# Batch 0's q and k in rows of eight tokens: loads, transposes and ordering copies at the start of a fused attention and feed-forward kernel

## The chip, the cores and the metric

The kernel runs on one core of a Trainium2 chip. A core has five engines with queues of their own: TensorE (PE in the profile; its weight loads have a row of their own, PEld), VectorE (DVE), ScalarE (ACT), GpSimd (POOL) and SyncE (SP), and 16 DMA engines that serve transfers issued from POOL, SP and ACT. The metric is the device time of one execution in microseconds (us). The kernel before takes 291.97 us, the median of three runs (291.71 to 292.54).

## The reference

For each of 8 batches and 8 heads there are 576 tokens of 64 values. Scores are masked to a causal window: heads 0 to 3 see the last 32 tokens, heads 4 to 7 ("dilated") every fourth token of the last 128. Softmax, product with v, and then a feed-forward layer over all 4608 tokens:

```
rel = pos[:, None] - pos[None, :]
mask_plain = (rel >= 0) & (rel < 32)
mask_dil = (rel >= 0) & (rel < 128) & (rel % 4 == 0)
attn = softmax(where(mask, q @ k.T / 8, -1e9))      # per batch and head
x = (attn @ v) moved to [4608 tokens, 512]
out = relu(x @ w_in) ** 2 @ w_out                    # 512 -> 2048 -> 512
```

Inputs and output are float32; the kernel computes in bfloat16, and its loads through POOL's queue convert on the way.

## The kernel before, in words

Attention of one batch and the feed-forward products of earlier tokens are interleaved. TensorE is the engine that is kept busy: nearly all of its time goes into the feed-forward products (`mm1`, line 912, with w_in; lines 960 and 997 with w_out), which start as soon as the first 256 tokens of attention output stand in the tile `xT`.

The order of all work is written by hand. The string `PROGRAM` (line 22 on) is read code by code by `run` (line 1147); what stands before its first `|` is issued before any feed-forward group, and each `|` is one feed-forward group further. Every engine runs its instructions in the order in which they were issued and waits on semaphores; a wait holds up all that is queued behind it on that engine.

Batch 0 has its own path, `first_step` (line 678). Its heads come in four pairs e = 0 to 3 (pairs 2 and 3 are dilated) and its tokens in two parts: part 0 is tokens 0 to 255, part 1 tokens 256 to 575. The codes used here:

- `L0:q001` loads part 0 of q and then of k for pairs 0 and 1, through `load_qk` (line 190), on POOL's queue. One row of the staging tile (`rb[0]`, tiles `qb` and `kb` in the profile) holds four consecutive tokens per head: partition p has tokens 4p to 4p+3, 64 partitions for part 0 and 80 for part 1. The order of loads is q001, q023, q123, v0d (two loads of v), i0 (the first quarter of w_in), q101, more of v, i1, more of v, i2, i3 and the four quarters of w_out. From the ninth load on, each waits until the load eight places ahead of it has landed.
- `T e part` (line 706) turns the rows into columns on TensorE: for q and for k, for each of the four tokens r of a row and both heads of the pair, one weight load of 64 or 80 rows by 64 values and one matmul with the identity, 16 transposes in all, into a PSUM tile [128, q or k, r, token/4]. `T20q` and `T20k` are its halves.
- `C e part` (lines 713 to 721) copies that PSUM tile to `xx[0]`: q in the order [r][m] (token 4m + r), k in the same order for the dilated pairs, and for the plain pairs in token order. The letter a or v after the code names ScalarE or VectorE. Because r is the outer index in PSUM too, the copies of line 713 and of line 720 read and write runs of neighbouring elements; that of line 721 does not read so. Line 715 copies the last 64 keys into `k8`.
- `B`, `S`, `E` are the mask added in PSUM (line 736), the scores (line 758) and the exponential (line 766, and the mask on VectorE, line 769); `P`, `D` the product with v and the sums (lines 796, 812); `L`, `X`, `M` the reciprocal of the sums by logarithm and exponential (lines 819, 822 on ScalarE) and the product with it into `xT` (line 829 on VectorE). `G` spreads v (line 255).
- `w` and `W` are products of zeros of 512 or 256 columns (`turn`, line 676) that change no result; they stand at fixed places in TensorE's order.
- `R` (line 925) empties the first two PSUM accumulators of `mm1`, which were held back.
- `y` clears rows 64 to 79 of the staging tiles of batch 1 (`rb[1]`) and of batches 0 and 2 (`rb[0]`), two memsets on POOL each, lines 1150 and 1151.

The plain and dilated pairs of part 0 go first (T00, T10, T20, T30), then part 1 of the dilated pairs (T21, T31), the first two feed-forward groups, then T01 and T11.

Of the kernel before, what the change touches and what calls it, by code (L numbers as in the profile page):

```python
# [12 lines left out]
RES = 4  # L13
# [68 lines left out]
def kernel(  # L82
# [9 lines left out]
    nc = tc.nc  # L92
    P = nc.NUM_PARTITIONS
# [58 lines left out]
    s2 = const.tile([P, HF, HT], bf16, name="s2T")  # L152
    osb = const.tile([P, NT // P, DM], f32, name="osb")
    slots = [0]
    rb = [{nm: const.tile([80, 2 * H * RES * D], bf16, name=f"{nm}b{i}") for nm in "qk"} for i in range(3)]
    qT = const.tile([P, NE, RES, M], bf16, name="qT")

    xx = [const.tile([P, 2, H * 2 * M], bf16, name=f"xx{i}") for i in range(2)]
# [27 lines left out]
    def staged(b: int, nm: str):  # L186


        t = rb[STAGE[b]][nm]
        return t[:, :].rearrange("p (a h x) -> p a h x", h=H, a=2)  # L190

    def load_qk(b: int, part, es):
        hs = slice(2 * es[0], 2 * es[-1] + 2)
# [486 lines left out]
    def first_step(code: str):  # L680
# [16 lines left out]
        if what == "T":  # L697
            if code[3:] != "k":
                ps = ps_a.tile([P, 1024], bf16, name="pa")
                first["T", e, part] = ps[:, 0 : 2 * w].rearrange("p (x r m) -> p x r m", x=2, r=RES)  # L700
            x = first["T", e, part]
            for z, nm in [(z, nm) for z, nm in enumerate("qk") if code[3:] in ("", nm)]:
                t = staged(0, nm)
                for r in range(RES):
                    for hl, rows in enumerate(sides):
                        nc.tensor.transpose(
                            x[rows, z, r, :], t[0:n, part, 2 * e + hl, D * r : D * r + D], ident[0:n, 0:n]
                        )
        elif what == "C":
            copy = nc.scalar.copy if code[3] == "a" else nc.vector.tensor_copy  # L710
            x = first.pop(("T", e, part))
            if dil:
                copy(qk0[:, :, e, :, m0 : m0 + n], x)
                if part:
                    nc.vector.tensor_copy(
                        k8[:, e - NE // 2, :].rearrange("p (m r) -> p m r", r=RES),
                        x[:, 1, :, n - 16 : n].rearrange("p r m -> p m r"),
                    )
            else:
                copy(qk0[:, 0, e, :, m0 : m0 + n], x[:, 0, :, :])  # L720
                nc.vector.tensor_copy(
                    xx[0][:, 1, S * e + RES * m0 : S * e + w + RES * m0].rearrange("p (m r) -> p m r", r=RES),
                    x[:, 1, :, :].rearrange("p r m -> p m r"),
                )
        elif what == "B":
# [421 lines left out]
    def run(code):  # L1147
        if code == "y":
            for nm in "qk":
                nc.gpsimd.memset(staged(1, nm)[64:80, 0, :, :], 0.0)  # L1150
                nc.gpsimd.memset(staged(2, nm)[64:80, 0, 0 : H // 2, :], 0.0)
        elif code == "z":
            nc.gpsimd.memset(vbd[1][0:64, :, :, 64:128], 0.0)
            nc.gpsimd.memset(vbd[1][64:128, :, :, 0:64], 0.0)
        elif code in "mu":
            masks(int(code == "u"))
        elif code == "R":
            while held:
                held.pop(0)()
        elif code == "N":  # L1160
            zero_halves(vbd[0][:, NE // 2 :, 0:8, :])
        elif code[0] == "G":
            spread_v(0, int(code[1]), [int(code[2])], nc.scalar.copy if code[3:] else nc.vector.tensor_copy)
        elif code == "h":
            for rows in sides:
                nc.vector.tensor_copy(vbd[0][rows, 0:2, 0:4, rows], plain[rows, :, :, :])
        elif code == "n":
            zero_halves(kbd)
            nc.sync.dma_start(mask_n[:, :], near_dram.ap())
        elif code[0] in "wW":  # L1170
            n, _, at = code[1:].partition("+")
            turn(int(n), 512 if code[0] == "w" else 256, [int(x) for x in at])
        elif code[0] in "TCBSEPDXM" or code[0] == "L" and code[2:3] != ":":
            first_step(code)
        elif code[0] != "L":
            step(int(code[0]), code[1:])
        else:
            b, what, part, which = int(code[1]), code[3], code[4:5], code[5:]
            if what == "V":
                load_v_rows(b, code[4:] or "d01")  # L1180
                return
            if what == "q":
                load_qk(b, None if part == "w" else int(part), [int(e) for e in which])
            elif what == "x":
                cross_all(b)
            elif what == "v":
                load_v(b, [0, 1] if part == "w" else [int(part)], which)
            else:
                (load_w_in if what == "i" else load_w_out)(int(part))
# [100 lines left out]
```

## Time and profile before

| what | value |
|---|---|
| median of three runs | 291.97 us |
| the profiled execution's own time | 292.3 us |
| its span, first to last instruction | 290.5 us |
| TensorE clock granted | 1.0 throughout |
| TensorE busy, 0 to 4.6 us / 4.6 to 8 / 8 to 12 | 3.53 / 3.08 / 3.50 us |
| 12 to 16 / 16 to 20 / 20 to 24 / 24 to 28 us | 3.02 / 3.94 / 2.64 / 3.93 us |
| 28 to 40 us / 40 to 80 / 80 to 160 / 160 to 290 us | 11.95 / 39.73 / 79.35 / 125.99 us |
| mean busy share of the DMA engines, 3 to 28 us in 40 slices | 0.8 or more in all but one |

The profile is of one execution. A row of its timeline gives the start, the time taken, the engine, the line of the kernel, the operation with the tiles written and read, a count where rows were merged, and in brackets the idle time of the engine just before and what ended it. "issue" as the cause means that nothing which the profile shows was waited for. From 28 us on, TensorE idles very little until near the end, so that a shift of the work at 28 us is a shift of the end unless something later absorbs it. Within the first 28 us TensorE is idle about 4 us in all, in a handful of places.

### The profile page before, as it was taken

What the parts mean: (1) busy time and instruction counts of PE and PEld (TensorE: products, weight loads), DVE (VectorE), ACT (ScalarE), POOL (GpSimd) and SP (SyncE); (2) the same over time, 40 slices, a digit from 0 to 9 for tenths busy, and PEclk for the clock granted to TensorE, in tenths of its full rate; (3) what the DMA queues carried; (4) which work ended last, traced back from release to release, by engine and by line L of the source; (5) the groups of instructions that cost most, each with busy time, mean ns of one, the idle gap of its engine ahead of it and who ended that gap; (6) DMA issues with size and microseconds to landing.
All of it is one profiled execution on the core that took longest, in us unless ns stands there. A gap on an engine that the chain in (4) does not pass through costs nothing.

```text
span 290.5 us, 8181 instructions
## 1 busy us (share of the span) xinstructions
PE 280.7 (97%) x3321; PEld 200.4 (69%) x3341; DVE 207.0 (71%) x447; ACT 194.7 (67%) x419; POOL 130.0 (45%) x210
## 2 busy tenths in 40 slices
PE   8879999999999999999999999999999999999994
PEld 3569855977955578557865786578657865885683
DVE  2565496798877997869786978697869545742762
ACT  7688748877986886597669766976697456306610
POOL 8569965393892779584043467950000000000000
PEclk9999999999999999999999999999999999999999
DMA  7999999999999987999789998740310040013013
GB/s 112 200 158 212 210 159 201 211 157 200 164 152 179 153 113 80 230 207 132 97 146 215 164 162 163 82 27 2 101 47 2 2 148 0 0 47 100 0 38 108
DMA packets 83125, 35.45 MB, mean 122 GB/s; under 512 B 52624, under 2 KB 78480, under 8 KB 83088
## 3 DMA queue, kind: packets, MB, share of 16 engines
q0 software_dynamic: 49280, 18.43, 55.9%
q1 hardware_dynamic: 33008, 16.10, 27.9%
q10 hardware_dynamic: 800, 0.41, 0.6%
q8 instruction: 26, 0.43, 0.6%
q14 instruction: 11, 0.09, 0.1%
HBM read 37.40 MB, written 9.44 MB: 161 GB/s over the span
## 4 chain that ended last, share of the span: by engine, by line
PE 88%; DMA 5%; DVE 2%; POOL 2%; issue 1%; ACT 1%; ACTq 0%; POOLq 0%
PE pf L912 41%; PE pf L997 29%; PE pf L960 8%; DMA w_in<-in_moe_w_in_dram 3%; DMA kb<-in_k_dram 2%; PE po L621 2%; PE pa L621 1%; PE pa L284 1%; PE pf L621 1%; PE pd L621 1%; POOL qb L197 1%; PE pa L358 1%; PE po L421 1%; DVE kbd L507 1%; PE pd L423 0%
## 5 line engine op out<-in xcount | busy, mean ns | idle before, releaser
L912 PE MATMUL pf<-xT,w_in 128*128 128x512 bf16 (+1 forms) x693 | 128.7, 340 | 2.1 <-DMA w_in<-in_moe_w_in_dram 1.4
L912 PEld LDWEIGHTS <-w_in 128*128 128x128 bf16 x704 | 77.4, 113 | 46.1 <-DMA w_in<-in_moe_w_in_dram 1.5
L925 ACT ACTIVATE h2T<-pf 128x512 bf16<-128x512 f32 x144 | 83.0, 600 | 36.7 <-PE pf L912 36.4
L997 PEld LDWEIGHTS <-h2T 128*128 128x128 bf16 x688 | 65.3, 98 | 9.1
L997 PE MATMUL pf<-w_out_sb,h2T 128*128 128x256 bf16 x440 | 52.3, 273 | 0.0
L483 POOL DMA_DIRECT2D vbd<-in_v_dram x80 | 43.4, 564 | 13.6 <-DMA qb<-in_q_dram 4.2
L889 DVE TENSOR_TENSOR h2T<-h2T 128x2048 bf16<-128x2048 bf16 (+2 forms) x42 | 35.6, 867 | 16.2 <-ACT h2T L925 15.6
L1008 DVE TENSOR_TENSOR osb<-pf,osb 128x512 f32<-128x512 f32 (+1 forms) x35 | 23.5, 673 | 12.6 <-PE pf L997 11.8
L960 PE MATMUL pf<-w_out_sb,h2T 128*128 128x512 bf16 x119 | 29.5, 379 | 0.6 <-issue 0.3
L647 DVE TENSOR_TENSOR xT<-po,rec 128x512 bf16<-128x512 f32 x16 | 11.0, 688 | 15.8 <-ACT rec L644 11.2
L197 POOL DMA_DIRECT2D qb<-in_q_dram x18 | 13.1, 730 | 16.3 <-DMA xx<-qb 15.0
L960 PEld LDWEIGHTS <-h2T 128*128 128x128 bf16 x128 | 11.4, 98 | 10.8
L930 DVE TENSOR_TENSOR h2T<-h2T 128x1024 bf16<-128x1024 bf16 (+1 forms) x20 | 11.5, 585 | 7.7 <-ACT h2T L925 7.2
L658 ACT ACTIVATE pt<-pa 128x384 bf16<-128x384 f32 (+1 forms) x32 | 15.3, 496 | 1.7 <-DVE xT L649 1.1
L475 POOL DMA_DIRECT2D vbd<-in_v_dram x20 | 12.3, 626 | 8.4 <-DMA kb<-in_k_dram 4.2
L644 ACT ACTIVATE rec<-rec 128x576 f32<-128x576 f32 x22 | 15.0, 682 | 0.5
L218 POOL DMA_DIRECT2D vbd<-in_v_dram x16 | 10.9, 690 | 9.7 <-DMA kb<-in_k_dram 4.4
L470 POOL DMA_DIRECT2D vd<-in_v_dram x20 | 12.3, 623 | 4.0 <-DMA kb<-in_k_dram 3.1
L997 PE MATMUL pf<-w_diff,s2T 128*128 128x256 bf16 x112 | 13.7, 273 | 0.0
L997 PE MATMUL pf<-vbd,h2T 128*128 128x256 bf16 x112 | 13.4, 273 | 0.0
L197 POOL DMA_DIRECT2D kb<-in_k_dram x18 | 13.0, 722 | 0.7 <-DMA vd<-in_v_dram 0.7
L997 PE MATMUL pf<-w_diff,h2T 128*128 128x256 bf16 x104 | 13.3, 273 | 0.0
(160 smaller groups left out, 416.6 us busy)
## 6 DMA issues: line engine op xcount, KB each, us to landing
out_dram<-osb SPq DMA_DIRECT2D x18, 128.0 KB, 5.8
qb<-in_q_dram POOLq DMA_DIRECT2D x7, 320.0 KB, 8.1
kb<-in_k_dram POOLq DMA_DIRECT2D x7, 320.0 KB, 10.3
vd<-in_v_dram POOLq DMA_DIRECT2D x32, 64.0 KB, 6.9
w_in<-in_moe_w_in_dram POOLq DMA_DIRECT2D x4, 512.0 KB, 8.4
w_out_sb<-in_moe_w_out_dram POOLq DMA_DIRECT2D x4, 512.0 KB, 11.0
qb<-in_q_dram POOLq DMA_DIRECT2D x7, 256.0 KB, 7.0
kb<-in_k_dram POOLq DMA_DIRECT2D x7, 256.0 KB, 12.3
```

The costliest lines, as they stand in the source:

```text
L197: nc.gpsimd.dma_start(t[0:n, part, hs, :], src[b, hs, t0 : t0 + RES * n, :].rearrange("h (p r) d -> p h (r d)", r=RES))
L470: nc.gpsimd.dma_start(vds[b][rows, e, :, :], v[b, H // 2 + 2 * e + hl, 0:512, :].rearrange("(m p r) d -> p m (r d)", p=64, r=RES),)
L483: nc.gpsimd.dma_start(v_rows[b % 2][p0 + 16 * r : p0 + 16 * r + 16, e, :, :], v[b, 2 * e + hl, :, :].rearrange("(i m r) d -> r m i d", r=R ...
L621: nc.tensor.matmul(out, lhs, rhs, start=begin, stop=True, skip_group_check=True)
L644: nc.scalar.activation(rec[:, :], rec[:, :], ACT.Exp, scale=-1.0)
L658: nc.scalar.activation(pt, sp[b, e][g][:, 0:n], ACT.Exp, scale=SCALE)
L889: nc.vector.tensor_tensor(out=hv, in0=hv, in1=hv, op=ALU.mult)
L912: nc.tensor.matmul(to, w_in_sb[piece][:, kt, c0 : c0 + 509 : 4], rhs, start=(kt == kts[0] and x == 0), stop=(kt == kts[-1] and x == per - ...
L925: nc.scalar.activation(hv, acc[u][:, :].rearrange("p (x n) -> p x n", x=2), ACT.Relu)
L960: nc.tensor.matmul(cur[m][:, :], h2[:, m // 2 if per == 1 else hh, HF * (f % 2) + f // 2, P * x : P * x + P], w_out_sb[:, f, :], start=(f ...
L997: nc.tensor.matmul(bank(nm, m, c.start)[:, m, c], a[:, k, P * m : P * m + P], w[:, c], start=begins, stop=(k == HF - 1), skip_group_check= ...
L1008: nc.vector.tensor_tensor(out=to[:, at, c], in0=src[:, at, c], in1=other[:, at, c], op=ALU.add)
```

## The change

Batch 0's q and k are staged in rows of eight tokens per head. A load of part 0 has 32 rows and one of part 1 has 40, four heads each, and one run in memory is 2 KB of float32 where it was 1 KB. The rows of the dilated pairs are placed on partitions 64 and up, those of the plain pairs on partitions 0 and up, so that the staging tiles are 128 partitions high instead of 80. The transposes take 32 or 40 rows, and there are eight of them where there were four for each head of q and of k. The PSUM tile has the order [q or k][r of 8][token/8]; token 8m + 4s + r' has to go to residue r' and place 2m + s, so the copies write every second element. Clearing rows 64 to 79 of `rb[0]` overlaps batch 0's dilated rows now; it is taken out of `y` and stands as `Y` behind the loads of batch 1's second part and ahead of the loads of batch 2. Number and order of the instructions of VectorE, ScalarE and SyncE are the same; POOL has its two memsets later; TensorE has 256 instructions more (128 weight loads, 128 matmuls).

```diff
-    "X21 M21 L31 X31 M31 E01 E11 | L2:q00123 L2:q10123 L1:v1dpr | | P01 D01 ...
+    "X21 M21 L31 X31 M31 E01 E11 | Y L2:q00123 L2:q10123 L1:v1dpr | | P01 D01 ...
...
-    rb = [{nm: const.tile([80, 2 * H * RES * D], bf16, name=f"{nm}b{i}") for nm in "qk"} for i in range(3)]
+    rb = [{nm: const.tile([P, 2 * H * RES * D], bf16, name=f"{nm}b{i}") for nm in "qk"} for i in range(3)]
...
+    def rows8(nm: str, e: int, part: int):
+        n, r0 = MN[part] // 2, 64 * int(e >= NE // 2)
+        c = 4 * RES * 2 * D
+        return slice(r0, r0 + n), rb[0][nm][r0 : r0 + n, c * part : c * part + c].rearrange("p (h x) -> p h x", h=4)
+
+    def load_first(part: int, es):
+        hs = slice(2 * es[0], 2 * es[-1] + 2)
+        for nm, src in (("q", q), ("k", k)):
+            rows, t = rows8(nm, es[0], part)
+            n, t0 = rows.stop - rows.start, RES * MS[part]
+            nc.gpsimd.dma_start(t, src[0, hs, t0 : t0 + 8 * n, :].rearrange("h (p r) d -> p h (r d)", r=8))
...
-                t = staged(0, nm)
-                for r in range(RES):
+                at, t = rows8(nm, e, part)
+                for r in range(8):
                     for hl, rows in enumerate(sides):
                         nc.tensor.transpose(
-                            x[rows, z, r, :], t[0:n, part, 2 * e + hl, D * r : D * r + D], ident[0:n, 0:n]
+                            x[rows, z, r, :], t[:, (2 * e + hl) % 4, D * r : D * r + D], ident[at, at]
                         )
...
+            mixed = x.rearrange("p x (s r) m -> p x s r m", s=2)
             if dil:
-                copy(qk0[:, :, e, :, m0 : m0 + n], x)
+                copy(qk0[:, :, e, :, m0 : m0 + n].rearrange("p x r (m s) -> p x s r m", s=2), mixed)
...
-                copy(qk0[:, 0, e, :, m0 : m0 + n], x[:, 0, :, :])
+                copy(qk0[:, 0, e, :, m0 : m0 + n].rearrange("p r (m s) -> p s r m", s=2), mixed[:, 0])
...
         if code == "y":
             for nm in "qk":
                 nc.gpsimd.memset(staged(1, nm)[64:80, 0, :, :], 0.0)
+        elif code == "Y":
+            for nm in "qk":
                 nc.gpsimd.memset(staged(2, nm)[64:80, 0, 0 : H // 2, :], 0.0)
...
-                load_qk(b, None if part == "w" else int(part), [int(e) for e in which])
+                (load_qk if b else lambda b, *x: load_first(*x))(b, int(part), [int(e) for e in which])
```

More of the change, by code (lines that the diff above doesn't have):

```diff
@@ L699, in first_step @@
                 ps = ps_a.tile([P, 1024], bf16, name="pa")
-                first["T", e, part] = ps[:, 0 : 2 * w].rearrange("p (x r m) -> p x r m", x=2, r=RES)
+                first["T", e, part] = ps[:, 0 : 2 * w].rearrange("p (x r m) -> p x r m", x=2, r=8)
             x = first["T", e, part]
             for z, nm in [(z, nm) for z, nm in enumerate("qk") if code[3:] in ("", nm)]:
-                t = staged(0, nm)
-                for r in range(RES):
+                at, t = rows8(nm, e, part)
+                for r in range(8):
                     for hl, rows in enumerate(sides):
                         nc.tensor.transpose(
-                            x[rows, z, r, :], t[0:n, part, 2 * e + hl, D * r : D * r + D], ident[0:n, 0:n]
+                            x[rows, z, r, :], t[:, (2 * e + hl) % 4, D * r : D * r + D], ident[at, at]
                         )
@@ L711, in first_step @@
             x = first.pop(("T", e, part))
+            mixed = x.rearrange("p x (s r) m -> p x s r m", s=2)
             if dil:
-                copy(qk0[:, :, e, :, m0 : m0 + n], x)
+                copy(qk0[:, :, e, :, m0 : m0 + n].rearrange("p x r (m s) -> p x s r m", s=2), mixed)
                 if part:
                     nc.vector.tensor_copy(
-                        k8[:, e - NE // 2, :].rearrange("p (m r) -> p m r", r=RES),
-                        x[:, 1, :, n - 16 : n].rearrange("p r m -> p m r"),
+                        k8[:, e - NE // 2, :].rearrange("p (m r) -> p m r", r=8),
+                        x[:, 1, :, n // 2 - 8 : n // 2].rearrange("p r m -> p m r"),
                     )
             else:
-                copy(qk0[:, 0, e, :, m0 : m0 + n], x[:, 0, :, :])
+                copy(qk0[:, 0, e, :, m0 : m0 + n].rearrange("p r (m s) -> p s r m", s=2), mixed[:, 0])
                 nc.vector.tensor_copy(
-                    xx[0][:, 1, S * e + RES * m0 : S * e + w + RES * m0].rearrange("p (m r) -> p m r", r=RES),
+                    xx[0][:, 1, S * e + RES * m0 : S * e + w + RES * m0].rearrange("p (m r) -> p m r", r=8),
                     x[:, 1, :, :].rearrange("p r m -> p m r"),
```

2 rows, old and new, of the table PROGRAM are left out of this document.

## The prediction

> **What bounds the kernel now.** I read the page's busy times first.
>
> ```profile
> PE 280.7 (97%) x3321; PEld 200.4 (69%) x3341; DVE 207.0 (71%) x447; ACT 194.7 (67%) x419; POOL 130.0 (45%) x210
> ...
> q8 instruction: 26, 0.43, 0.6%
> ```
>
> TensorE is the bound, so the question is how much it idles where the change works, in the first 28 us. Its waits from 0 to 60 us, then, of the longest pieces of the chain of work, four:
>
> ```profile
> PE pf L912 <- DMA w_in<-in_moe_w_in_dram: 1.4, 1, 1.4
> ...
> PE pf L758 <- issue: 1.0, 1, 1.0
> PE pa L706 <- DMA kb<-in_k_dram: 0.8, 2, 0.5
> ```
>
> ```profile
> 12.90 8.41 DMA w_in<-in_moe_w_in_dram
> ...
> 21.36 1.95 PE pf L912 x16
> ...
> 26.46 0.50 DVE xT L829
> ...
> 27.00 7.91 PE pf L912 x71
> ```
>
> The reader should see three places: a load of w_in that lands at 21.3 us ends 1.4 us of idling; the k loads end 0.8 us; and 1.0 us, ahead of a score matmul, has no cause named but "issue". From 27.0 us on TensorE goes without a pause, released by the last product into xT. The wait called issue, from the weight loads' timeline, and the DMA view of the stretch from 12.97 to 13.00 us:
>
> ```profile
> 9.18 0.21 PEld L706 LDWEIGHTS <-kb 64*64 64x64 bf16 x8
> ...
> 15.23 0.10 PEld L758 LDWEIGHTS <-kbd 64*64 64x64 bf16 x1 [1.10 <-issue]
> ```
>
> ```profile
> q8 instruction: 1, 0.02, 203.1%
> ```
>
> Queue q8 carries instructions: 26 packets, 0.43 MB, 16 KB each. The page has 3321 + 3341 = 6662 TensorE instructions, 256 to a packet, so q8 is TensorE's program arriving in blocks of 256 (128 weight loads with their matmuls). Counted in the program's order, the load that stalls until 15.23 us is number 224, the load at 9.18 us number 96: one block apart. I read it so: two blocks are held, the end of one asks for the next but one, and TensorE stands still if it runs through a block sooner than that arrives. Asked at 9.18 us, seen on the queue at 12.98, usable at 15.23: 6.05 us. The second packet starts at 19.08, again 3.85 us after its block end at 15.23.
>
> **The change, part by part.** DMA. In the 1.0 us from 37 to 38 us the load queue moved 375 packets of 512 bytes (389 less 14 small ones), in that from 25 to 26 us 204 packets of 1024 bytes:
>
> ```profile
> DMA packets 390, 0.21 MB, mean 208 GB/s; under 512 B 15, under 2 KB 389, under 8 KB 389
> ```
>
> ```profile
> DMA packets 204, 0.21 MB, mean 209 GB/s; under 512 B 0, under 2 KB 204, under 8 KB 204
> ```
>
> With 16 engines, 43 ns and 78 ns per packet and engine. Batch 0's q and k are 8 x 144 x 2 / 16 = 144 packets per engine, 6.2 us; as 72 of double size, 5.6 us. The loads gain 0.5 us by the time that the w_in quarter of 21.3 us lands, if they spread evenly over the engines. The issues on POOL cost 0.64 us per load of 256 runs (2.61 us), 0.60 for 128 (v, 9.17 us): nothing, since POOL then waits for landings anyway.
>
> TensorE. 128 more transposes. Groups of eight follow each other by 0.13 us (9.05, 9.18) at 64 columns and by 0.14 at 80 (17.58, 17.72), 17 ns each; the 16 score matmuls of 13.47 us, 32 and 80 columns mixed, take 0.29 us, 18 ns. So I take no saving from 32 or 40 columns: +0.14 us for each of 16 groups, 2.2 us. Lower bound: price by columns, nothing.
>
> Copies. Writing every second element should cost VectorE its faster rate:
>
> ```profile
> L721 DVE COPY xx<-pa 128x320 bf16<-128x320 bf16 x2 | 0.9, 486 | 0.0
> ...
> L721 DVE COPY xx<-pa 128x256 bf16<-128x256 bf16 x2 | 0.8, 420 | 2.7 <-ACT xx L720 2.7
> ...
> L713 DVE COPY xx<-pa 128x512 bf16<-128x512 bf16 x2 | 0.8, 418 | 1.4 <-PE pa L706 1.4
> ...
> L713 DVE COPY xx<-pa 128x640 bf16<-128x640 bf16 x1 | 0.5, 492 | 0.3 <-PE pa L706 0.3
> ```
>
> Line 721, already strided, pays 66 ns for 64 elements; line 713 pays 74 for 128. At line 721's rate C20 and C30 take 0.68 us (+0.27), C21 0.82 (+0.32), C01 0.49 (0.33 before). At best, nothing. ScalarE's copies (376 ns for 256, 692 for 640) are at one rate already; I leave them.
>
> Y. Two memsets of 0.94 us (30.38, 33.02) move behind the two loads issued at 39.23 and 40.65 and ahead of four issued from 41.36, and eight loads from 33.92 come 1.9 us sooner. Cover: the DMA engines are 0.9 busy there, so the queue has work while POOL clears. Cost 0; uncovered, a first packet late by up to 1.9 us for a batch used 20 us later.
>
> The block ends. 256 more instructions are exactly one block, so from weight load 480 on all blocks end where they did; ahead of that they end at other work. Load 96 is now the seventh of S10's eight, at 7.1 to 7.2 us (they stand from 7.07), 2 us sooner. Load 224 is the sixth transpose of T31's q. When does TensorE get there? T20q at 7.84; with doubled groups and the three `w` behind it T20k at 9.03 (8.93 before); T30 to 9.8; C20 at 9.5 to 10.15, so S20 at 10.4; C30 to 10.8, S30 at 11.0; T21 from 11.25 (its k landed at 11.45 before, some 0.4 sooner now); T31q at 11.75, load 224 at 11.85. The block asked for at 7.1 is usable at 7.1 + 6.05 = 13.15. A stall of 1.3 us, where 1.0 us at 15.23 goes.
>
> The sum. T31's other 27 transposes, 0.46 us: P00 at 13.7 (12.04 before, +1.65). M00 and M20 ended at 14.92 and 16.01, now 16.55 and 17.65. The first feed-forward group, 15.61 to 17.45, needs M00 for its first half and M20 for its second: T01 from 18.7 (+1.25). Load 352 is the fifteenth of T01q, 18.95; its block, asked for at 13.15, comes at 19.2. Then three doubled groups, 0.85 us: P21 at 20.1 (18.14, +1.95). ScalarE runs from C11 (18.43) to the third `h2T` eviction (22.46) practically without a gap, so this goes through: the evictions at 24.35 and, waiting for nothing now, 24.95 (22.46 and 23.33 before); L01 at 25.5 (24.66); the last xT product ends at 27.75 (26.95), and TensorE's long run begins at 27.8, not 27.0. **+0.8 us.** The profiled execution (292.3 us, span 290.5) would be 293.1 with a span of 291.3; it stands 0.3 above the median of 291.97, which becomes 292.8.
>
> The row of 15.23 us shows a stall of 0.98 us at a block end. [...]
>
> **The rivals.** First: the third block is late as well. Its 6.05 us would run from 19.2 to 25.25, while TensorE reaches load 480, among the sums of pair 1, at about 24.6; L01 and what follows move by another 0.6: +1.4, 293.4. Against it: the third block before was asked for at 24.16 and on the queue at 27.16, 0.8 us quicker.
>
> Second: the block comes in time, which needs less than 4.7 us from 7.1 to 11.85. Then T31 ends 0.35 us later than before, the stall at 15.23 is gone, T01 starts as before, P21 at 18.6; the w_in quarter lands at 20.8 and no longer counts, but ScalarE's row does: the run starts at 26.5: -0.5, 291.5. For it: T20 stands 2 us earlier, when fewer loads are queued; against it: 3.80 and 3.85 us on the queue, twice alike.
>
> Third, the other side: the block is in time and transposes are priced by columns (8 ns). Then P21 comes at 17.9, S11 ends at 19.7, and the w_in quarter at 20.8 decides: -1.1, 290.9. It takes over where a transpose costs under 10 ns. The rows of 13.47 us, 18 ns, speak against it.
>
> 40 rows do not divide by 16 as 64 and 80 do, and no load of before has such a number; if a third of the engines took more than their share, the 0.5 us of loads would be gone, and the third rival would end near -0.5. [...]
>
> **How the numbers follow.** Forecast 0.48, first rival 0.18, second 0.18, third 0.16. The forecast's own range, for 0.5 us on the block's arrival either way, is 292.3 to 293.3. About 0.3% (0.88 us) is what a measurement of this kernel can tell from no change: half of the forecast lies beyond it (0.24) with all of the first rival: slower 0.42. The other half and most of the second (0.14): same 0.38. The rest, faster 0.20. The range, 291.0 to 294.0, takes in the second rival and the first with its 0.5 us; half of the third stays below, something above.
>
> **What would show it.** A stall of over 0.8 us called issue inside T31's q near 12 us, none at the last score matmul of S31; q8's first packet near 11 us, its second near 17; T01 near 18.7; the w_in wait gone and TensorE's run from 27.8. Transposes of 32 columns 17 ns apart; C20 near 0.68 us. Wrong if the first q8 packet comes under 3 us after S10, if a 40-row load lands much later than 1 us behind the one before it, or if the run at 27 us moves and the end does not.

## The result, and the profile after

The changed kernel takes 294.49 us (median of six runs, 293.71 to 295.28) against 291.84 us for the kernel before on the same chip: a ratio of 1.0083, 95% interval 1.0063 to 1.0104. Forecast were 292.8 us, 291.0 to 294.0. The sign was right, the size was not: +2.65 us instead of +0.8. Three more measurements of the same kernel gave ratios of 1.0066, 1.0083 and 1.0079; over all 28 undisturbed executions the median is 294.28 us. A few executions of several kernels are disturbed, up to 11 us longer than the others of the same kernel; they are left out of every ratio and of the medians called undisturbed, and two profiles that fell on such executions are not read.

The page of the profiled execution (293.71 us, span 291.9), busy times and the instruction queue:

```profile
PE 284.8 (98%) x3449; PEld 203.1 (70%) x3469; DVE 208.0 (71%) x447; ACT 194.5 (67%) x419; POOL 129.2 (44%) x210
...
q8 instruction: 27, 0.44, 0.6%
```

128 matmuls, 128 weight loads and one packet of instructions more, as the order says. TensorE's waits from 0 to 60 us (total, times, longest) are now only these:

```profile
PE po L690 <- DVE kbd L1106: 1.1, 1, 1.1
PE pf L927 <- DVE xT L844: 0.4, 1, 0.4
```

All three waits of the kernel before are gone, and no standstill stands in T31's q either. Yet the chain of waits from 27 us on says that the long run starts 1.7 us later than before:

```profile
28.14 0.50 DVE xT L844
...
28.68 7.91 PE pf L927 x71
```

The timeline of TensorE shows why nothing waited (start, time taken, line, tiles):

```profile
1.07 4.45 PE L690 MATMUL po<-kbd 128*128 128x512 bf16 x10 [1.07 <-DVE kbd L1106]
5.45 0.60 PE L720 MATMUL pa<-mk,qb 32*64 32x32 bf16 x16
...
10.64 0.42 PE L720 MATMUL pa<-mk,qb 32*64 32x32 bf16 x16
```

The ten zero products stand 0.43 us apart to the last (in the kernel before from 3.9 us on 0.22), and sixteen transposes take 0.43 us from one group to the next until 7.2 us, 0.26 from 11.75 on. TensorE ran at half pace until about 10 us, though the profile's column of the granted clock says 1.0 there. The trace itself agrees with the pace: its rows of granted clock begin only at 10.46 us in this execution, at 3.77 us in the first profile of the kernel before, and the column shows 1.0 wherever there is no row. T20 comes at 10.64, not 7.84; weight load 96 at 9.53, not 7.1. So this one execution is not the one that I forecast. I needed more profiles of it.

### The profile page after: what moved, and what is told of

Same layout as the page of the kernel before. It is cut to its first block, busy times and chain, and to the rows that moved or that the text cites. A ratio compares the mean times of both kernels' runs of the same rounds, so it can differ in the third digit from the quotient of the medians.

```text
span 291.9 us, 8438 instructions
## 1 busy us (share of the span) xinstructions
PE 284.8 (98%) x3449; PEld 203.1 (70%) x3469; DVE 208.0 (71%) x447; ACT 194.5 (67%) x419; POOL 129.2 (44%) x210
## 4 chain that ended last, share of the span: by engine, by line
PE 95%; ACT 1%; DVE 1%; issue 1%; ACTq 0%
PE pf L927 42%; PE pf L1012 29%; PE pf L975 9%; PE po L690 2%; PE pa L720 2%; PE po L635 2%; PE pa L635 1%; PE pa L298 1%; PE pf L635 1%; PE pd L635 1%; PE pf L773 1%; DVE xT L844 1%; ACT h2T L940 1%; PE pa L372 1%; PE po L435 1%
## 5 line engine op out<-in xcount | busy, mean ns | idle before, releaser
L211 POOL DMA_DIRECT2D qb<-in_q_dram x14 | 10.2, 729 | 16.0 <-DMA xx<-qb 15.3
L1012 PE MATMUL pf<-vbd,h2T 128*128 128x256 bf16 x112 | 13.4, 273 | 0.0
L648 ACT ACTIVATE rec<-pd 128x512 f32<-128x512 f32 x6 | 3.6, 597 | 13.4 <-PE pf L635 13.4
```

Of the source, the lines that this page charges most:

```text
L1012: nc.tensor.matmul(bank(nm, m, c.start)[:, m, c], a[:, k, P * m : P * m + P], w[:, c], start=begins, stop=(k == HF - 1), skip_group_check= ...
```

## The experiments

### The same kernels again: is the slow start the cause?

Edit: none.

> The changed kernel once more, unaltered. In its first profile TensorE's early zero products of 512 columns stand 0.43 us apart up to 5.5 us and the 32-row transposes take 0.42 us per 16 up to 7.2 us; both have the pace of a full clock (0.22 us and 0.26 us) only from about 10.6 us on, where the kernel before had it from 3.9 us on. Theory A, the slow start belongs to the changed work: it is here again, full pace from about 10 us, T20 at 10.5 to 10.7, TensorE's long run from 28.5 to 28.8, time 293.5 to 295.3. Theory B, the slow start was chance of that one execution: full pace from 4 us here, T20 at about 7.9, and then what I forecast must show, a wait called issue of about 1.3 us near 12 us, long run from about 27.8, while the time is again 293.5 to 295.3 and has to be explained otherwise.

> The kernel before once more, unaltered. Theory A (the slow start belongs to the changed work): full pace from about 4 us again, T20 at 7.9, wait called issue of about 1 us at the last score product of S31, long run from 27.0. Theory B (chance of an execution): the slow start up to about 10 us can turn up here too, with T20 near 10.5, and the time then hardly differs from the 291.4 to 292.5 of the other runs, or it would have shown in them.

Measured: changed kernel 294.00 us (undisturbed median), ratio 1.0066 [1.0046, 1.0086]; before 291.58 us, ratio 1.0005 [0.9978, 1.0033]. The changed kernel's second profile (294.14 us), TensorE's timeline:

```profile
1.07 3.94 PE L690 MATMUL po<-kbd 128*128 128x512 bf16 x10 [1.07 <-DVE kbd L1106]
...
8.24 0.42 PE L720 MATMUL pa<-mk,qb 32*64 32x32 bf16 x16
...
13.68 0.34 PE L720 MATMUL pa<-mk,qb 40*64 40x40 bf16 x11 [1.50 <-issue]
```

Full pace from 4.5 us, and there is the standstill of the forecast: it begins after the fifth or sixth transpose of T31's q (forecast: load 224, the sixth), lasts 1.50 us (1.3) and ends at 13.68 (13.15). The first instruction packet is at 11.18 us (forecast near 11). Theory A, the slow start as the cause, falls: this execution has none and takes as long. But the standstill alone is not enough either, because the long run starts at 28.89, not 27.8 (chain of work):

```profile
28.35 0.50 DVE xT L844
...
28.89 7.91 PE pf L927 x71
```

The windows of the same profile (busy time of PE, PEld, DVE, ACT, POOL with counts, then the granted clock, DMA share, GB/s):

```profile
12.00:14.00 2.00, 0.50 (x32) 0.40 (x28) 1.39 (x3) 0.00 (x0) 1.93 (x3) 1.00 1.24 202
14.00:16.00 2.00, 2.00 (x52) 1.64 (x46) 0.73 (x4) 1.57 (x3) 0.00 (x0) 0.65 1.38 179
16.00:18.00 2.00, 2.00 (x40) 1.39 (x39) 1.36 (x4) 1.97 (x4) 1.81 (x3) 0.50 1.35 204
18.00:20.00 2.00, 2.00 (x29) 1.77 (x29) 1.66 (x5) 1.41 (x4) 2.00 (x4) 0.99 1.45 142
```

Behind the standstill the granted clock is 0.5, in finer windows from 14.6 to 18.0 us. The kernel before, profiled again, has its standstill of 1.10 us at S31's last product, and a clock of 1.00 behind it:

```profile
15.09 0.21 PE L758 MATMUL pf<-xx,kbd 64*64 64x64 bf16 x1 [1.10 <-issue]
```

### Doubled transposes alone

In the kernel before, each transpose is issued twice; loads, layout and copies stay:

```
-                for r in range(RES):
+                for r in [y // 2 for y in range(2 * RES)]:
```

> The kernel before with each of batch 0's transposes issued twice in a row (256 TensorE instructions more, at the same places as in the changed kernel); loads, layout and copies are those of before, and the result is the same. My forecast's theory, the doubled transposes and the block ends moved by them: 16 transposes take about 0.27 us, T20k at 9.0, a wait called issue of over 0.8 us inside T31's q near 12 us, none at S31's last product, long run from 27.6 to 28.1, +0.5 to +1.2 us. Theory A (the doubled transposes, which fill the stretch from 4.6 to 7 us, keep TensorE slow): slow until about 10 us, T20 from about 10.3, long run from 28.3 or later, +1.5 to +2.7 us. Theory C (the cost comes with the loads and the copies, the transposes cost only themselves): full pace from 4 us, no long wait, +0 to +0.4 us.

Measured: 294.14 us, ratio 1.0075 [1.0045, 1.0105]. That is as much as the whole loss, without a load, a layout or a copy changed, and more than the +0.5 to +1.2 us that my forecast's theory gave it. Theory C falls. Its profile is of one of its quickest executions (292.81 us); timeline and chain:

```profile
13.41 0.38 PE L706 MATMUL pa<-mk,qb 80*64 80x80 bf16 x11 [0.71 <-issue]
```

```profile
27.25 0.50 DVE xT L829
...
27.79 2.23 PE pf L912 x19
```

Standstill in T31's q, no stretch at half clock behind it, long run at 27.79: this is close to the execution that I forecast (27.8; 293.1 for a profiled execution). The way there differs: the standstill is 0.71 us and not 1.3, because load 224 is reached at 12.47 and not 11.85, and each later step is 0.3 to 0.4 us late until the last, which I had put 0.4 us too long. So the forecast's course exists, but it is the best case, not the usual one, and its hitting 27.8 is in part luck.

### The copies alone

In the kernel before, the copies of lines 713 and 720 go through every second element, in both operands:

```
+            mixed = x.rearrange("p x r (m s) -> p x s r m", s=2)
-                copy(qk0[:, :, e, :, m0 : m0 + n], x)
+                copy(qk0[:, :, e, :, m0 : m0 + n].rearrange("p x r (m s) -> p x s r m", s=2), mixed)
```

> The kernel before with its copies of the transposed q and k (lines 713 and 720) writing and reading every second element, as the changed kernel's copies write; loads and transposes are those of before. In the profiles of the changed kernel VectorE's copy of 512 elements took 0.72 us instead of 0.42, of 640 0.87 instead of 0.49, and ScalarE's of 640 0.87 instead of 0.69. My forecast: these lie beside waits (the k load, the program's arrival at 15.2 us, w_in), and alone they cost 0 to +0.3 us: 291.7 to 292.1. Rival: C20, C30 and C21 delay the scores one after the other and C31 the eviction behind it, +0.5 to +1.0 us; the equal times of the changed kernel and of doubled transposes alone (294.07 and 294.14) would then have to come from a gain of the larger loads of the same size.

Measured: 291.53 us, ratio 0.9985 [0.9969, 1.0000]. The copies got as slow as in the changed kernel (groups of its profile: busy time and mean ns of one, then idle before):

```profile
L714 DVE COPY xx<-pa 128x512 bf16<-128x512 bf16 x2 | 1.3, 719 | 1.3 <-PE pa L706 1.3
...
L714 ACT COPY xx<-pa 128x640 bf16<-128x640 bf16 x1 | 0.9, 887 | 0.9 <-PE pa L706 0.9
```

and in this kernel that cost nothing. The last product into xT starts at 26.09 here, at 25.81 in the repeated kernel before, and at 26.46 in its first profile. TensorE has no standstill at S31's last product in this profile: it came there later, so that what the copies took could come out of that wait. So the run shows the price in the kernel before, with its waits; in the changed kernel it is argued from doubling alone, which is as slow without them.

### Rows of eight for part 0 alone

Part 1 is loaded, transposed and copied as before: no loads of 40 rows, 64 transposes more instead of 128.

```
-                (load_qk if b else lambda b, *x: load_first(*x))(b, int(part), ...)
+                (load_qk if b or int(part) else lambda b, *x: load_first(*x))(b, int(part), ...)
```

> The changed kernel with rows of eight tokens for part 0 alone: part 1 is loaded in rows of four (80 rows), transposed and copied as in the kernel before, so there are no loads of 40 rows and 64 more transposes instead of 128. Theory C (40-row loads that land unevenly, and the slower copies of part 1): the w_in quarter i0 lands by 15.5 us instead of 16.5, and most of the loss is gone, 0 to +0.7 us against before. Theory A (slow start from the transposes of 32 rows): T00 to T30 are as in the changed kernel, so TensorE is slow until about 10 us here too and 1.2 us or more of the loss stays, +1.2 to +2.3 us. My forecast's theory: 128 instructions more, so block ends move by half a block; a wait called issue stands at another place, and the total is between -0.3 and +0.8 us.

> Rows of eight tokens for part 0 alone, once more, for a profile; its time was 293.04 us, ratio 1.0034. Block mechanism: the 96th load stays in S10 near 7.5 us, the 224th is now in P00 (64 loads fewer ahead of it in T21 and T31 than a doubling of all gives, 32 of them), reached near 12.0 to 12.4; arrival at 13.6 to 13.9; a standstill of 1.2 to 1.8 us in P00, long run 0.5 to 1.0 us earlier than in the changed kernel, 292.8 to 293.7. Theory C, kept as a rival (loads of 40 rows, slower copies of part 1 make most of the loss): no standstill over 1 us and a w_in quarter i0 that lands by 15.5 us.

Measured: ratio 1.0034 [1.0016, 1.0052] and, the second time, 1.0013 [0.9996, 1.0031]; undisturbed medians 292.74 and 292.42 us. In the profile of the second (293.26 us) the standstill is where the count of loads puts it, in P00, behind the 224th load:

```profile
13.94 0.28 PE L829 MATMUL pf<-pt,vbd 128*128 128x96 bf16 x3 [1.07 <-issue]
```

Half of the added transposes cost a sixth to two fifths of the loss, and the smaller figure is not clear of nothing. As the loads of 40 rows are gone too, this run does not separate the two; doubling alone does.

### Filling the standstill

Three zero products more behind T20's q, and, after that failed, seven ahead of T21:

```
-    "w3 T20k ..."        (first)        -    "... S30 E30 T21 ..."        (second)
+    "w6 T20k ..."                       +    "... S30 E30 w7 T21 ..."
```

> The changed kernel with three more zero products of 512 columns (0.22 us each) behind T20's q, where three stand already: 0.65 us of work for nothing, which changes no result. In the second profile of the changed kernel TensorE stood still from 12.17 to 13.68 us, waiting for its program, and its granted clock was 0.5 from 14.6 to 18.05 us; in the kernel with doubled transposes alone, where it stood still for 0.71 us, no such stretch followed. Theory D, the standstill of 1.5 us is what lowers the clock: with the standstill shortened to about 0.85 us by products that run in its place, its end stays near 13.7 us, the stretch at half clock is gone from most executions (mean granted clock 0.996 to 1.0 instead of 0.988 to 0.994), and the time falls by 0.5 to 1.3 us to 292.7 to 293.5: more work, less time. Theory E, the stretch at half clock has nothing to do with the standstill: it stays, and the time is as before the edit or 0.1 to 0.7 us longer, 294.0 to 294.8.

Measured: 294.59 us, ratio 1.0082 [1.0055, 1.0110]; nothing gained, and clocks of 0.988 to 1.0. Not a test of theory D, because the standstill did not shrink: the block came later, 6.8 us after its load 96.

```profile
14.48 0.40 PE L720 MATMUL pa<-mk,qb 40*64 40x40 bf16 x14 [1.65 <-issue]
```

> The changed kernel with seven more zero products of 512 columns (1.5 us in all) ahead of T21, behind the score products of pair 3. Three zero products behind T20's q did not do what was meant: the program arrived 0.8 us later in that profile, and the standstill was 1.65 us again. The changed kernel stands still in T31's q for 1.3 to 1.65 us until 13.7 to 14.2 us, and in all profiles with a standstill of 1.17 us or more (two kernels, five profiles) the granted clock was 0.5 for 3.4 us behind it; in those with 1.1 us or less (five profiles) never. Theory D, the standstill brings the half clock: TensorE now works until about 13 us, the standstill (seven weight loads earlier in the old count, at T21's end) is 0.2 to 0.7 us, half clock is gone from most executions, and the time falls by 0.5 to 1.2 us to 293.0 to 293.9, with 1.5 us more work. Theory E, the two only go together by chance: half clock as often as before the edit, and 294.0 to 295.5.

Measured: 293.97 us (undisturbed median), ratio 1.0071 [1.0045, 1.0098]. The profile (294.98 us), TensorE's timeline and two windows:

```profile
14.23 0.21 PE L720 MATMUL pa<-mk,kb 40*64 40x40 bf16 x2 [0.55 <-issue]
...
26.60 0.38 PE L927 MATMUL pf<-xT,w_in 128*128 128x256 bf16 x2 [0.82 <-issue]
```

```profile
14.00:16.00 2.00, 1.77 (x67) 1.63 (x67) 1.08 (x3) 1.02 (x2) 0.34 (x1) 1.00 1.31 187
16.00:18.00 2.00, 1.51 (x44) 0.99 (x41) 1.74 (x6) 1.94 (x4) 1.79 (x3) 1.00 1.37 198
```

The standstill is down to 0.55 us and the clock stays at 1.00. The mean granted clock, which a stretch of 3.4 us at one half lowers by 0.006, is 0.997 or more in all six undisturbed executions; of the 28 of the kernel without this edit only seven are above 0.995, fifteen are at 0.991 to 0.994, as with one stretch, and six at 0.988, as with two. So the half clock comes with the long standstill. The time forecast with it did not come: the undisturbed median is 293.97 against 294.28, so 1.5 us of useless products cost nothing, but they bring 0.3 at most, which lies within the two intervals. What is saved is waited for again at 26.60 us: the next block but one is late now, by 0.82 us.

### Cutting the zero products at the start

The ten zero products shrink from 512 columns to 128, in both kernels; the count of instructions stays.

```
+        if n == 10:
+            cols, rhs = 128, idle[:, 0:128]
```

> The changed kernel with its ten zero products at the start cut from 512 to 128 columns each, same number of instructions: they end near 2.2 us instead of 4.9 to 5.5, and TensorE then idles until the first load lands. In the first profile of the changed kernel TensorE ran at half pace up to about 10 us, although the page says 1.0 there. Theory A, the zero products are what brings the full pace, and chance decides whether they do: here the slow start is certain, T20 comes at 9.5 to 10.7, the program arrives in time so that no wait called issue stands in T31's q, the long run starts at 28.0 to 28.8, time 293.2 to 294.5 with a narrower spread. Theory B, the pace at the start does not hang on them: T00 starts at 4.5 at full pace, wait called issue of 1.5 us as in the second profile, time 293.5 to 294.5.

> The kernel before with the same cut of its ten first zero products. Theory A with room to spare: the slow start is certain, T20 comes near 9.5 to 10 instead of 7.9, but the kernel before had waits of 1.0 us (issue, 15.2 us) and 1.4 us (w_in, 21.3 us) in its first profile, which take up most of it: long run from 27.0 to 27.5, time +0 to +0.5 us, 291.8 to 292.3. Theory A without room: ScalarE's row of work behind T01 moves by the whole 1.5 to 2 us and the time is 1 to 2 us longer, 292.8 to 293.8; then the kernel before cannot have had slow starts in its ordinary executions, most of which lie between 291.2 and 292.4. Theory B: no change, 291.6 to 292.0.

Measured: the changed kernel 1.0089 [1.0053, 1.0126] (no profile of it is read, so how it starts is not shown), the kernel before 1.0011 [0.9992, 1.0029], 292.32 us. The kernel before, TensorE's timeline:

```profile
4.51 0.42 PE L709 MATMUL pa<-mk,qb 64*64 64x64 bf16 x8 [2.19 <-DMA qb<-in_q_dram]
...
9.24 0.31 PE L709 MATMUL pa<-mk,qb 64*64 64x64 bf16 x8
...
15.55 0.21 PE L761 MATMUL pf<-xx,kbd 64*64 64x64 bf16 x1 [0.68 <-issue]
```

The slow start is here (T20 at 9.24 instead of 7.88; the rows of granted clock begin at 8.96 us), and the kernel before takes it without a loss clear of noise: its standstill shrinks from about 1.0 to 0.68 us, and the last product into xT starts at 25.92. The kernel before has room at its start, and forgives most of what the first 10 us lose.

### The other profiles of the changed kernel and of doubling alone

Edit: none.

> The changed kernel a third time, for its profile. In all eight profiles of undisturbed executions so far the time is the start of the last product into xT (25.81 to 29.33 us) plus 265.56 to 265.84 us; here again. Theory F, three things set that start in the changed kernel: the standstill of 1.5 to 1.65 us in T31's q that I forecast, a stretch of 3.4 us at half clock behind it (14.6 to 18.05 us in the second profile), or instead of both a slow start up to about 10 us: an execution of 293.5 to 294.5 shows one of the last two, one with the standstill alone is at 292.5 to 293.2. Rival G: something that neither profile showed; an execution above 293.5 us without a slow start and without a stretch at half clock.

> The changed kernel a fourth time, for its profile; the same expectations as for the third: theory F, over 293.5 us only with a slow start past 8 us or a stretch of 3.4 us at half clock, and 292.5 to 293.2 with the standstill alone; rival G, over 293.5 us with neither.

> The kernel with doubled transposes alone a second time, for its profile. Its first showed full pace from about 4 us, a standstill of 0.71 us and 292.81 us, though the median of its executions is 294.14 and nearly all show a mean granted clock of 1.0. Theory F: an execution above 293.5 us has the slow start, past 8 us, no or a short standstill, and the last product into xT starts later than 27.9 us. Rival G: full pace from 4 to 5 us and no stretch at half clock, and still above 293.5, by a wait that the first profile did not have (the third block of the program, or a load).

> Doubled transposes alone a third time, for its profile; the same expectations as for the second: theory F, above 293.5 us only with a slow start past 8 us; rival G, above it at full pace, by a wait that the first profile did not have.

Measured: 1.0083 [1.0053, 1.0113], 1.0079 [1.0047, 1.0110], 1.0064 [1.0041, 1.0088], 1.0075 [1.0054, 1.0095]. Both profiles of the changed kernel have the standstill and the half clock, as theory F says. So has the first of the two others (293.85 us, standstill 1.17 us), and neither theory written for it foresaw that: one had a slow start, the other no half clock. The last, 293.78 us with a clock of 1.0 and no slow start, is rival G's:

```profile
13.62 0.38 PE L706 MATMUL pa<-mk,qb 80*64 80x80 bf16 x11 [0.64 <-issue]
...
19.89 0.23 PE L706 MATMUL pa<-mk,qb 80*64 80x80 bf16 x2 [0.24 <-issue]
```

A second standstill stands at T01's q, the block end after the first. The weight loads of the changed kernel's fourth profile (294.62 us) show one at the third, in P01:

```profile
26.63 0.10 PEld L811 LDWEIGHTS <-vbd 128*128 128x128 bf16 x1 [0.28 <-issue]
```

Counting the weight loads in the order of each trace puts the profiles of these two kernels and of doubling alone into one table. "96" and "352" are the starts of these loads, "225" and "481" of the first load of the block after the next. In the kernel before, the load that stalls is 224 and stands in the column of 225; load 353 does the work of 481, and its block stood on the queue at 19.08 us in the first profile and has long come. Elsewhere the stalled load is 225, 352, 479 or 480, so the count is good to two loads:

| profile | 96 | 225 | 352 | 481 | last product into xT | time |
|---|---|---|---|---|---|---|
| before, first | 9.18 | 15.23 | | 24.23 | 26.46 | 292.30 |
| before, again | 9.25 | 15.09 | | 23.57 | 25.81 | 291.38 |
| forecast for the change | 7.15 | 13.15 | 18.95 | 24.65 | 27.25 | 293.1 |
| changed, first (slow start) | 9.53 | 14.27, no wait | 20.19 | 25.91 | 28.14 | 293.71 |
| changed, second | 7.53 | 13.68 | 20.00 | 26.12 | 28.35 | 294.14 |
| changed, third | 8.05 | 13.92 | 20.47 | 26.19 | 28.42 | 294.27 |
| changed, fourth | 8.03 | 14.19 | 20.65 | 26.67 | 28.90 | 294.62 |
| doubling alone, first | 7.47 | 13.41 | 19.23 | 25.02 | 27.25 | 292.81 |
| doubling alone, second | 7.68 | 13.66 | 20.17 | 25.95 | 28.18 | 293.85 |
| doubling alone, third | 8.18 | 13.62 | 19.89 | 25.86 | 28.08 | 293.78 |

Behind load 481 every measured row is the same: 2.2 us to the last product into xT, and 265.6 to 265.9 us from its start to the time. Everything that the change costs in these executions is there by load 481, in the first 27 us.

### Moving the block ends

Two of the ten first zero products become 30 tiny ones: 28 weight loads more ahead of all work.

```
+        if n == 10:
+            n = 8
+            for _ in range(30):
+                nc.tensor.matmul(to[0:64, 0:32], idle[0:64, 0:64], idle[0:64, 0:32], ...)
```

> The kernel before with two of its ten first zero products replaced by 30 tiny ones (64 rows by 64 values, 32 columns): 28 weight loads and 28 matmuls more ahead of everything, in about the time of the two. The 96th load, whose block end asks for the next block, is then one among the zero products at 7.5 us instead of the first of T30's k at 9.2 us; the 224th is the sixth of S21 instead of S31's last. My forecast's block mechanism (about 6.05 us from block end to arrival, half of it ahead of the packet): first q8 packet near 11.3 us instead of 12.7 to 13.0, arrival at 13.5 to 13.7, a standstill of 0.2 to 0.5 us in S21 near 13.3 us instead of 1.0 to 1.1 us at S31's last product near 14.1, first feed-forward product about 0.5 us earlier, time 0 to 0.7 us less, 291.1 to 291.8. Rival: the wait called issue is not the program's arrival but belongs to S31's last product: it stays there with 1.0 us, and the time stays at 291.6 to 292.0.

> The changed kernel with the same 28 more tiny loads and products at the start. Block mechanism: the 96th load is now in T10's k at 5.9 to 6.5 us, arrival at 12.0 to 12.6; the 224th is at S30 or T21's first ten, reached near 11.4, so the standstill shrinks from 1.3 to 1.65 us to 0.6 to 1.1 us; but the 352nd load is now the third of the first feed-forward group, reached near 16 us, and its block, asked for near 12.1 to 12.6, comes at 18.1 to 18.7: a standstill of 1.5 to 2.5 us where there was none, and one of about 1 us more in S11 near 23 us. Time 294.5 to 296.5. Rival (the waits belong to the places, not to the count of loads): standstill in T31's q as before and none in the first feed-forward group, 294 to 294.7.

Measured: the kernel before 291.75 us, ratio 1.0003 [0.9983, 1.0024]; the changed kernel 297.53 us (median of three undisturbed executions, 296.62 to 299.34), ratio 1.0196 [1.0156, 1.0237], more than the 294.5 to 296.5 expected. Of the kernel before, all TensorE waits up to 40 us:

```profile
PE po L677 <- DVE kbd L1097: 1.1, 1, 1.1
PE pf L918 <- DMA w_in<-in_moe_w_in_dram: 0.5, 1, 0.5
PE pf L918 <- DVE xT L835: 0.3, 1, 0.3
```

The standstill is gone from S31's last product, and the 0.2 to 0.5 us expected in S21 are not there either. That alone does not show that it belonged to the count of loads and not to S31: the tiny products took 1.7 us instead of 0.9 and TensorE was at half pace until about 8.6 us, T20 came at 9.89, and a late TensorE alone shrinks the standstill (0.68 us with T20 at 9.24 above). The same list of the changed kernel settles it. It has two new standstills, ahead of the third product of the first feed-forward group and of the second product of the second, behind S11, where the count puts loads 352 and 480:

```profile
PE pf L933 <- issue: 2.3, 2, 1.4
PE pa L726 <- issue: 1.6, 1, 1.6
```

They last 0.96 and 1.35 us. Places and sign are those of the block mechanism. One number is not: load 96 stood at 6.77 us here, and the block came at 13.99, after 7.2 us instead of 6.05, so that the standstill at T21's q is 1.56 us and not the 0.6 to 1.1 expected.

## Why the prediction was wrong, point by point

**DMA.** The gain on the loads is there behind the loads of 32 rows and gone behind those of 40. In the four profiles of the changed kernel k of the dilated pairs landed at 7.74 to 8.05 us (8.89 in the first profile of before), but T21's k, which I had put 0.4 us sooner, landed at 11.60 to 11.99 (TensorE's wait for it ended at 11.49 before). My sign for this came: the two loads of 40 rows landed 1.6 to 2.2 us behind the one issued before them on POOL's queue, those of 80 rows 1.1 to 1.5. The time shows neither the gain nor its loss: doubling alone, with the old loads, is as slow (undisturbed medians 293.96 and 294.28 us). Which engines carried the 40 rows is in no row that I read, so whether they were spread unevenly stays open.

**TensorE's transposes.** Right: 16 of 32 rows follow each other in 0.26 us, 16 to 17 ns each, the same as 64 rows (0.27 in the doubling alone). The rival that priced them by columns falls.

**Copies.** Sizes right for VectorE (512 elements 0.72 us for 0.68, 640 0.87 for 0.82); wrong for ScalarE, which I left alone: 640 elements 692 to 873 ns, 256 elements 376 to 440. That they cost nothing was right, and is shown by the copies alone for the kernel before.

**Y.** Nothing in the start or behind it hangs on it; I found no wait for it and did not test it by itself.

**The block ends.** The mechanism was right in place and kind: T31's q, the sixth transpose, in all six read profiles of the changed kernel and of doubling alone without a slow start to 10 us. Its duration of 6.05 us lies in the middle of what was measured, 5.1 to 7.2 us, but it is no fixed time from load 96, as the sum took it. Nine of the ten profiles of kernels with doubled transposes that were read show standstills of 0.55 to 1.65 us at a block end.

**The sum** failed, at three terms, which can be read from the table against the forecast's own row:

- From load 96 to 225: load 96 at 7.1 us and a fixed 6.05 us behind it, arrival 13.15; measured 13.4 to 14.2 us where TensorE waited for it, +0.3 to +1.0. Load 96 itself was late. I carried over the start of the one profile of before, where the zero products sped up at 3.9 us and T00 started at 4.65; in the other twelve read profiles with these zero products T00 started at 4.83 to 5.45 us, in eight of them at 5.1 or later. But the arrival does not follow load 96: with load 96 at 6.77 us (moved block ends) the block came at 13.99, at 7.50 (seven fill products) at 14.23, at 8.18 (doubling alone, third) at 13.62. What failed is the fixed time from request to arrival.
- From 225 to 352: 5.8 us in the forecast and in the first profile of doubling alone (13.41 to 19.23), 6.3 to 6.6 us in the four profiles of the table with half clock (three of the changed kernel, the second of doubling alone): +0.5 to +0.8. The half clock I did not see at all. It is not the only way to this lateness: doubling alone, third profile, took 6.27 us at full clock, because its second block came late. And most of the loss does not need it: 18 of the 24 executions of doubling alone have a mean granted clock above 0.995, and their median is 293.9 us.
- From 352 to 481: 5.7 to 5.8 us, when TensorE sets it; the third block takes 6.0 to 6.1, so +0.3 to +0.4 where it is late (second and fourth profile of the changed kernel, third of doubling alone). That is my first rival (0.18), and I had treated it as another case. It belongs to the same one: as I read the table, a block that arrives late also moves the next request, and TensorE needs about as long for a block (5.7 to 5.8 us) as a block needs to come (6.0 to 6.1).

For the second profile that is 0.53 + 0.52 + 0.42 = 1.47 us, from 24.65 to 26.12. The last step, from there to the long run, I had put 0.38 us too long (3.15 us; measured 2.77), so that the run starts 1.1 us later than forecast, at 28.89, and 293.1 us, the forecast for a profiled execution, becomes 294.2. The 0.3 us that I took off to get from the profile to the median was, as I read it, a fourth error: that profile was above its median because its long run started late (27.0 us; the last product into xT started 0.65 us earlier in the repeated one), and nothing says that the changed kernel inherits such a chance of the start.

The execution with the slow start took the same time by another way (481 at 25.91): it has no standstill, because TensorE is itself late. This fits with how little the zero products and the fill products changed the time: in this kernel, what is lost at one block end is not waited for at the next, and what is saved is waited for.

What stays open: what sets the arrival of a block. In all read profiles of kernels with doubled transposes the first packet stood at 11.1 to 11.8 us, whether load 96 was at 6.8 or at 9.5 us, and where TensorE waited for it the block was usable 2.2 to 2.7 us later. That looks like a queue behind the loads of the start; no run took loads away from it.

## What to carry to other kernels

Count instructions as a resource: where TensorE's program ran 256 instructions in less time than the next block took to come (here 5.1 to 7.2 us, while the loads of the start were under way), added small matmuls cost by the block ends that they moved, not by their own time: 28 tiny ones cost nothing in the kernel before and about 3 us in the changed one. Before summing from one profile, ask which of its intervals are fixed and which are chance: the 6.05 us read there from a block end to an arrival was 5.1 to 7.2 us elsewhere, and the start of T00 varied by 0.8 us. And a standstill of 1.17 us or more in the transposes had 3.41 us of half clock behind it, in all six profiles that show one; a sum should name it, though here most of the loss came without.

## What the runs showed of the hardware that was not expected

- The half clock. In all six read profiles with a standstill of 1.17 to 1.65 us in the transposes, the granted clock was 0.5 behind it, for 3.41 us each time (14.61 to 18.02 in the second profile of the changed kernel); in none of the read profiles where that first standstill was 1.10 us or less. It does not follow every pause of that length: the wait of 1.4 us for w_in in the first profile of before, and one of 1.35 us at 26.1 us in the changed kernel with moved block ends, had full clock behind them. The trace's rows of granted clock give a reason: they last 3.41 us or a multiple of it (full clock for 286.72 us, 84 times 3.413, in the first profile of before, and for 279.89 us, 82 times, in that of the changed kernel; 10.24 us from the first row to the half clock, in all six), so that I read the clock as settled once per step of 3.41 us. The two pauses that did nothing are each cut by the border of a step, counted from the first row, into 0.90 and 0.52 us and into 1.14 and 0.21; of each of the six standstills 1.17 us or more lies within one step. So 1.17 us of standstill in a step was enough here and 1.14 us was not; that idling alone decides is not shown.
- The slow start. Zero products of 512 columns stood 0.43 us apart at first and 0.22 later. The trace's first row of granted clock, which goes with that change of pace, came anywhere from 3.77 to 6.14 us where the ten zero products stood as they were, in one execution at 10.46, while the profile's clock column said 1.0. The pitch of equal products shows it, the column does not.
- 64 rows or 32 make no difference to a transpose's time (16 to 17 ns); half the rows means twice the time for the same data, and twice the program.
